# The first tile's key matmuls moved ahead of the second tile's transposes

## The chip, the cores and the metric

The kernel runs on one core of one Trainium2 chip. A core has five engines with instruction queues of their own: TensorE (matmuls, in the profile PE, with PEld for its weight loads), VectorE (DVE), ScalarE (ACT), GpSimd (POOL) and SyncE (SP, which here only issues transfers). Matmuls write to PSUM, which has 8 banks; VectorE and ScalarE carry results from there to SBUF. The metric is the device time of one execution in microseconds (us), as a median of several runs. The span of the profile is the time from the first to the last instruction, a little shorter.

## The reference, cut to what matters

The input `x` has 2048 rows (S) of 512 columns (D). The output is a gated sum of two branches of it:

```
q, k, v = x @ wqkv          # 32 heads of 16
phi(t)  = where(t > 0, t + 1, exp(t)) + 1e-6
kv      = phi(k)^T v        # per head, 16 x 16
z       = sum over rows of phi(k)
a       = (phi(q) kv) / (phi(q) . z + 1e-6) @ wo
h       = layernorm(x)
b       = (gelu(h^T @ w1 + b1) @ w2 + b2)^T      # mixes the rows
g       = sigmoid(sum(x * gate_w))
out     = g * a + (1 - g) * b
```

All inputs and the output are bf16. Of this, the change touches only how the first rows' keys `k = x @ wk` are started.

## The kernel before, in words

The rows are cut into 16 tiles of 128 (`NT`), the 512 columns into four chunks of 128 (`ND`). A matmul contracts over the partitions, so `k = x @ wk` needs x with its columns on the partitions: `xT`. For tiles 3 to 15 transposing DMAs (`load_xT`, L134) write `xT` directly. Those would come too late for the first three tiles (`HEADS = 3`), which TensorE transposes itself: `transpose_tile` (L202) multiplies each of the four 128x128 chunks of a tile with the identity, into one PSUM bank `pt`. VectorE then copies chunks 0 and 1 to `xT` (L209), and ScalarE chunks 2 and 3 (L210).

`k_part(t, ks)` (L224) runs the key matmuls of tile t for the chunks in `ks`; four of them, 128x128 by 128x512, add up to one bank `kacc`. `k_phi(t)` then calls `phi` (L212): an exp on ScalarE (L214), a min and an addition on VectorE (L215), and on VectorE again the sum with the positive part, which writes `pk` (L218). Next to these, `ln_step` takes the layer norm's statistics of a tile on VectorE (L238, L239).

The kernel is written under a manual schedule: each engine gets its instructions in the order of the calls in the program, and works them off in that order. An instruction waits for its inputs and for its output buffer, and whatever is behind it on the same engine waits with it. Tiles of PSUM come from one pool of 8 banks, in turn. The dependencies are kept per such tile; in the built program ScalarE's copy of `pt` waits for VectorE's copy of the same `pt`.

Loads: SyncE issues x's tiles 0, 1 and 2 one by one, then the transposing loads, the other tiles, and the weights; ScalarE issues the two halves of `wk` (chunks 0 and 1, chunks 2 and 3). Six matmuls on constants (`warm_up(6)`) keep TensorE at work until x's first tile is there.

The stretch around the change starts at L286: the transposes of tiles 0 and 1, the first two key matmuls of both, the transposes of tile 2, one `ln_step`, and then for tiles 0 to 2 the remaining key matmuls and the phi. After it comes the loop over tiles 3 to 15, in which the key matmuls of tile t alternate with `g_tile(t - 4)`, four matmuls of x against `pk` (`gacc`). Then follow the first products of the row mixing together with the queries (`uacc`, `qacc`), the rest of that product with the small attention matrices, and at last the output tiles (`aps`, `yps`).

Of the kernel before, what the change touches and what calls it, by code (L numbers as in the profile page):

```python
# [7 lines left out]
ACT = mybir.ActivationFunctionType  # L8
# [7 lines left out]
def kernel(  # L16
# [13 lines left out]
    nc = tc.nc  # L30
    P = nc.NUM_PARTITIONS
# [9 lines left out]
    ND = D // P  # L41
# [25 lines left out]
    def keep(shape, dtype, name):  # L67
        return persist.tile(shape, dtype, name=name, tag=name)

    def bank(name, dtype=FP32):  # L70
        return ps.tile([P, SC], dtype, name=name, tag="bank")

    xs = keep([P, NT, D], BF16, "xs")
    hs = keep([P, NT, D], BF16, "hs")
    xT = keep([P, ND, S], BF16, "xT")
# [17 lines left out]
    ident = keep([P, P], BF16, "ident")  # L93
# [18 lines left out]
    def mm(o, lhsT, rhs, start, stop, **kw):  # L112
        nc.tensor.matmul(o, lhsT=lhsT, rhs=rhs, start=start, stop=stop, **kw)  # L113
# [20 lines left out]
    def load_xT(t0, n):  # L134
# [14 lines left out]
        out=ident[:], in_=ident[:], compare_op=ALU.not_equal, fill=1.0, base=0,  # L149
# [5 lines left out]
        out=maskQ[:], in_=maskH[:].rearrange("p (a m) -> p m a", m=2), op=ALU.max, axis=AX.X  # L155
# [4 lines left out]
        out=xT[:, :, 3 * P : 3 * P + 2],  # L160
        in_=xs[:, 0, 0 : 2 * ND].rearrange("p (k c) -> p k c", k=ND),
# [10 lines left out]
    for c, (j0, nb) in enumerate(w1_chunks):  # L172
        w = wpool.tile([P, NT, FB * P], BF16, name="w1c", tag="wc")
        w1c.append(w)
        for t0 in range(0, NT, 8) if c < 3 else (0,):
            t1 = t0 + 8 if c < 3 else NT
            nc.sync.dma_start(
                out=w[:, t0:t1, : nb * P], in_=w1_view[:, t0:t1, j0 * P : (j0 + nb) * P]
# [15 lines left out]
    def warm_up(n, cols=SC):  # L194
        for _ in range(n):
            mm(wps[:, :cols], warm[:, 0:P], warm[:, :cols], True, True)
# [2 lines left out]
    nc.scalar.activation(out=act_warm[:], in_=ones_f[:], func=ACT.Exp)  # L199
    warm_up(6)  # L200

    def transpose_tile(t):  # L202
        pt = bank("pt")
        for k in range(ND):
            mm(pt[:, k * P : (k + 1) * P], xs[:, t, k * P : (k + 1) * P], ident[:], True, True)
        H = ND // 2
        src = pt[:].rearrange("p (k s) -> p k s", k=ND)
        dst = xT[:, :, t * P : (t + 1) * P]
        nc.vector.tensor_copy(out=dst[:, 0:H], in_=src[:, 0:H])  # L209
        nc.scalar.activation(out=dst[:, H:], in_=src[:, H:], func=ACT.Copy)  # L210

    def phi(dst, acc):  # L212
        e = work.tile([P, SC], BF16, name="e", tag="e", bufs=6)
        nc.scalar.activation(out=e[:], in_=acc[:], func=ACT.Exp)  # L214
        nc.vector.tensor_scalar(  # L215
            out=e[:], in0=e[:], scalar1=1.0, scalar2=PHI_EPS, op0=ALU.min, op1=ALU.add
        )
        nc.vector.scalar_tensor_tensor(  # L218
            out=dst, in0=acc[:], scalar=0.0, in1=e[:], op0=ALU.max, op1=ALU.add
        )  # L220
# [3 lines left out]
    def k_part(t, ks):  # L224
        if t not in kaccs:
            kaccs[t] = bank("kacc")
        for k in ks:
            mm(
                kaccs[t][:], xT[:, k, t * P : (t + 1) * P], wk_sb[:, k, :],
                k == 0, k == ND - 1,  # L230
            )

    def k_phi(t):
        phi(pk[:, t, :], kaccs.pop(t))
# [46 lines left out]
    def ln_step(u):  # L281
        ln_stats(u)
        if u % TPC == TPC - 1:
            ln_rstd(u // TPC)

    HEADS = 3  # L286
    transpose_tile(0)
    transpose_tile(1)
    for t in range(2):
        k_part(t, range(2))  # L290
    transpose_tile(2)
    ln_step(0)
    for t in range(HEADS):
        k_part(t, range(2 if t < 2 else 0, ND))
        k_phi(t)
    ln_step(1)
# [159 lines left out]
    for j in range(NB0, NF):  # L456
# [19 lines left out]
        out=gg[:], in0=gth[:], scalar1=0.5, scalar2=0.5, op0=ALU.mult, op1=ALU.add  # L476
    )
    nc.vector.tensor_scalar(
        out=c1[:], in0=gth[:], scalar1=-0.5, scalar2=0.5, op0=ALU.mult, op1=ALU.add
# [3 lines left out]
    for t in range(NT):  # L483
        c, tl = divmod(t, TPC)
        aps = bank("aps")
        for j in range(ND):
# [3 lines left out]
            out=a_sc[:], in_=aps[:], func=ACT.Identity,  # L490
            scale=gg[:, t : t + 1], bias=c2[:, t : t + 1],
        )
        for c0, W in ((0, D - P), (D - P, P)) if t == NT - 1 else ((0, D),):
            cs = slice(c0, c0 + W)
            yps = bank("yps")
            for f in range(NF):
# [6 lines left out]
                out=ot[:, :W], in0=yps[:, :W], scalar=c1[:, t : t + 1], in1=a_sc[:, cs],  # L503
# [35 lines left out]
```

## Time and profile before

| | |
|---|---|
| time, median of 3 runs | 164.42 us (164.37 to 164.69) |
| span of the profiled execution | 162.3 us |
| TensorE busy | 157.4 us, 97% |
| VectorE busy | 89.8 us, 55% |
| ScalarE busy | 63.1 us, 39% |
| landing of x's tiles 0, 1, 2 after their issue | 2.4, 3.1, 4.0 us |
| landing of the two halves of wk after their issue | 3.2, 3.8 us |
| granted TensorE clock | 1.0 |

How to read it: busy is the time in which an engine has at least one instruction under way. Matmuls are pipelined, so a row of them that starts every 0.216 us shows 0.38 us for each; the distance of the starts is what each costs in a dense row. The chain that ended last is followed back from the last instruction, at each step to what released it; its time stretches are the ones that set the end. In a timeline the brackets at the end of a line give the idle time of the engine ahead of it, and what ended it.

### The profile page before, as it was taken

To read this page: it belongs to the slowest core of one execution; us is meant where nothing else is said; L and a number is where in the kernel's file an instruction comes from. 1 tells how busy PE (TensorE), PEld (TensorE's weight loads), DVE (VectorE), ACT (ScalarE), POOL (GpSimd) and SP (SyncE) were. 2 spreads that over 40 slices of the span, in tenths; PEclk is the share of its full clock that TensorE was granted. 3 is DMA by queue.
4 is the path that set the end of the run, shared out by engine and by line. 5 is a ranking of instruction groups with operands and counts; after the bars stand their busy time and mean duration, and the time that the engine had idled before them with its cause. 6 is when DMAs were issued, how large, how long until landed. Compare 5 with 4: busy or idle time off the path is not lost.

```text
span 162.3 us, 2177 instructions
## 1 busy us (share of the span) xinstructions
PE 157.4 (97%) x819; PEld 72.2 (44%) x833; DVE 89.8 (55%) x212; ACT 63.1 (39%) x98; POOL 17.5 (11%) x34
## 2 busy tenths in 40 slices
PE   7899999999999999999999999999999999999993
PEld 2444444444444444444444444444444444444452
DVE  1699999967999999519995301256211111111112
ACT  3552294748677483112865113111122222111110
POOL 3000701200110000001415500050000000000000
DMA  5999999999910007600992699732000001110001
GB/s 156 239 220 231 277 321 325 379 385 386 358 30 0 0 0 233 219 4 0 284 325 88 201 326 313 278 128 71 32 32 32 32 32 42 48 43 33 32 32 32
DMA packets 30569, 25.18 MB, mean 155 GB/s; under 512 B 8480, under 2 KB 29984, under 8 KB 30560
## 3 DMA queue, kind: packets, MB, share of 16 engines
q1 hardware_dynamic: 28288, 21.89, 43.4%
q0 software_dynamic: 1440, 2.38, 5.4%
q10 hardware_dynamic: 832, 0.79, 1.5%
q8 instruction: 6, 0.10, 0.3%
q14 instruction: 3, 0.02, 0.0%
HBM read 21.11 MB, written 2.23 MB: 144 GB/s over the span
## 4 chain that ended last, share of the span: by engine, by line
PE 95%; DMA 2%; issue 1%; DVE 0%; SPq 0%
PE uacc L113 30%; PE yps L113 30%; PE gacc L113 8%; PE aps L113 8%; PE kacc L113 8%; PE qacc L113 8%; DMA xs<-in_A_x_dram 2%; PE denps L113 1%; PE pt L113 0%; PE kvps L113 0%; DVE xT L209 0%; SPq L129 0%; PE w2ps L113 0%; DVE ot L502 0%; PE pt L332 0%
## 5 line engine op out<-in xcount | busy, mean ns | idle before, releaser
L113 PE MATMUL uacc<-hs,w1c 128*128 128x512 bf16 x220 | 51.1, 379 | 0.2
L113 PE MATMUL yps<-uT,w2c 128*128 128x512 bf16 (+2 forms) x234 | 50.6, 366 | 0.2
L502 DVE SCALAR_TENSOR_TENSOR ot<-yps,c,a_sc 128x512 bf16<-128x512 f32 (+2 forms) x17 | 12.2, 719 | 44.7 <-PE yps L113 41.5
L113 PEld LDWEIGHTS <-w2c 128*128 128x128 bf16 x238 | 22.8, 98 | 25.9
L113 PEld LDWEIGHTS <-w1c 128*128 128x128 bf16 x224 | 21.8, 98 | 26.3 <-issue 0.2
L489 ACT ACTIVATE a_sc<-aps,c,gg 128x512 f32<-128x512 f32 x16 | 12.4, 777 | 46.7 <-PE aps L113 39.9
L326 ACT ACTIVATE uT<-uacc,bcol 128x512 bf16<-128x512 f32 x14 | 9.3, 688 | 21.7 <-PE uacc L113 21.7
L113 PE MATMUL qacc<-xT,wq_sb 128*128 128x512 bf16 x61 | 16.1, 379 | 0.2
L113 PE MATMUL aps<-W2sb,pqT 128*128 128x512 bf16 x63 | 16.2, 379 | 0.1
L113 PE MATMUL kacc<-wk_sb,xT 128*128 128x512 bf16 x63 | 16.1, 379 | 0.2
L113 PE MATMUL gacc<-pk,xs 128*128 128x512 bf16 x63 | 15.7, 379 | 0.0
L254 ACT ACTIVATE hs<-xs,nmr,rstd 128x512 bf16<-128x512 bf16 x16 | 12.8, 806 | 3.1 <-DVE nmr L248 3.1
L214 ACT ACTIVATE e<-qacc 128x512 bf16<-128x512 f32 x16 | 9.6, 597 | 9.2 <-PE qacc L113 9.2
L441 POOL DMA_DIRECT2D rex<-rd_dram x16 | 9.4, 601 | 22.5 <-DVE pqT L443 20.0
L214 ACT ACTIVATE e<-kacc 128x512 bf16<-128x512 f32 x16 | 9.3, 593 | 6.6 <-DVE mv L239 2.3
L218 DVE SCALAR_TENSOR_TENSOR pqT<-qacc,e 128x512 bf16<-128x512 f32 x16 | 11.1, 692 | 0.6
L218 DVE SCALAR_TENSOR_TENSOR pk<-kacc,e 128x512 bf16<-128x512 f32 x16 | 11.1, 692 | 0.6
L113 PEld LDWEIGHTS <-xs 128*128 128x128 bf16 x76 | 7.2, 100 | 9.4 <-DMA xs<-in_A_x_dram 1.6
L238 DVE BATCH_NORM_STATS2 stats<-xs 128x6 f32<-128x512 bf16 x16 | 10.9, 684 | 0.0
L215 DVE TENSOR_SCALAR e<-e 128x512 bf16<-128x512 bf16 x32 | 9.0, 281 | 2.3 <-ACT e L214 2.1
L428 DVE CUSTOM_DVE_ANT_0 junk<-xs,gw_b 128x512 bf16<-128x512 bf16 x16 | 9.8, 681 | 0.0
L279 DVE TENSOR_TENSOR zacc<-zacc,pk 128x512 f32<-128x512 f32 x14 | 9.6, 685 | 0.2
(61 smaller groups left out, 70.1 us busy)
## 6 DMA issues: line engine op xcount, KB each, us to landing
w1c<-in_B_w_dram SPq DMA_DIRECT2D x7, 1024.0 KB, 10.7
w2c<-in_B_w_dram SPq DMA_DIRECT2D x8, 896.0 KB, 5.9
rex<-rd_dram POOLq DMA_DIRECT2D x16, 128.0 KB, 4.0
out_dram<-ot SPq DMA_DIRECT2D x13, 128.0 KB, 1.7
xs<-in_A_x_dram SPq DMA_DIRECT2D x3, 512.0 KB, 4.6
wk_sb<-in_A_wqkv_dram ACTq DMA_DIRECT2D x2, 256.0 KB, 3.5
xs<-in_A_x_dram SPq DMA_DIRECT2D x4, 128.0 KB, 3.4
wq_sb<-in_A_wqkv_dram SPq DMA_DIRECT2D x1, 512.0 KB, 6.8
```

The costliest lines, as they stand in the source:

```text
L113: nc.tensor.matmul(o, lhsT=lhsT, rhs=rhs, start=start, stop=stop, **kw)
L214: nc.scalar.activation(out=e[:], in_=acc[:], func=ACT.Exp)
L215: nc.vector.tensor_scalar(out=e[:], in0=e[:], scalar1=1.0, scalar2=PHI_EPS, op0=ALU.min, op1=ALU.add)
L218: nc.vector.scalar_tensor_tensor(out=dst, in0=acc[:], scalar=0.0, in1=e[:], op0=ALU.max, op1=ALU.add)
L238: nc.vector.bn_stats(out=stats[:], in_=xs[:, t, :])
L254: nc.scalar.activation(out=hs[:, t, :], in_=xs[:, t, :], func=ACT.Identity, scale=rstd[:, t : t + 1], bias=nmr[:, t : t + 1],)
L279: nc.vector.tensor_tensor(out=zacc[:], in0=first, in1=pk[:, t, :], op=ALU.add)
L326: nc.scalar.activation(out=uT[:, j, :], in_=acc[:], func=ACT.Gelu_apprx_tanh, bias=bcol[:, j : j + 1])
L428: nc.vector.tensor_tensor_reduce(out=junk[:], in0=xs[:, t, :], in1=gw_b[:], scale=1.0, scalar=0.0, op0=ALU.mult, op1=ALU.add, accum_out=gp ...
L441: nc.gpsimd.dma_start(out=rex[:], in_=src.unsqueeze(1).to_broadcast([8, HEAD, SC]))
L489: nc.scalar.activation(out=a_sc[:], in_=aps[:], func=ACT.Identity, scale=gg[:, t : t + 1], bias=c2[:, t : t + 1],)
L502: nc.vector.scalar_tensor_tensor(out=ot[:, :W], in0=yps[:, :W], scalar=c1[:, t : t + 1], in1=a_sc[:, cs], op0=ALU.mult, op1=ALU.add,)
```

## The change

The change has three parts.

- `transpose_tile` is cut into `transpose_part`, which transposes a range of chunks into a bank of its own and copies it with one engine. A tile takes two banks where it took one, the first tile three.
- The first tile's chunks 0 and 1 are copied one by one by VectorE, so that the key matmul of chunk 0 need not wait for chunk 1.
- The order is another: the first two key matmuls of tile 0 come between the transposes of tiles 0 and 1; the other two, with the tile's phi, come ahead of the transposes of tile 2.

It is meant to give TensorE work while the second tile's rows are still under way, and to have the first phi early.

```diff
+    def transpose_part(t, k0, k1, on_act):
+        pt = bank("pt")
+        for k in range(k0, k1):
+            mm(pt[:, k * P : (k + 1) * P], xs[:, t, k * P : (k + 1) * P], ident[:], True, True)
+        src = pt[:, k0 * P : k1 * P].rearrange("p (k s) -> p k s", k=k1 - k0)
+        dst = xT[:, k0:k1, t * P : (t + 1) * P]
+        if on_act:
+            nc.scalar.activation(out=dst, in_=src, func=ACT.Copy)
+        else:
+            nc.vector.tensor_copy(out=dst, in_=src)
+
     def transpose_tile(t):
-        pt = bank("pt")
-        for k in range(ND):
-            mm(pt[:, k * P : (k + 1) * P], xs[:, t, k * P : (k + 1) * P], ident[:], True, True)
-        H = ND // 2
-        src = pt[:].rearrange("p (k s) -> p k s", k=ND)
-        dst = xT[:, :, t * P : (t + 1) * P]
-        nc.vector.tensor_copy(out=dst[:, 0:H], in_=src[:, 0:H])
-        nc.scalar.activation(out=dst[:, H:], in_=src[:, H:], func=ACT.Copy)
+        transpose_part(t, 0, ND // 2, False)
+        transpose_part(t, ND // 2, ND, True)
...
     HEADS = 3
-    transpose_tile(0)
+    transpose_part(0, 0, 1, False)
+    transpose_part(0, 1, 2, False)
+    transpose_part(0, 2, ND, True)
+    k_part(0, range(2))
     transpose_tile(1)
-    for t in range(2):
-        k_part(t, range(2))
+    k_part(1, range(2))
+    k_part(0, range(2, ND))
+    k_phi(0)
     transpose_tile(2)
     ln_step(0)
-    for t in range(HEADS):
+    for t in range(1, HEADS):
         k_part(t, range(2 if t < 2 else 0, ND))
         k_phi(t)
     ln_step(1)
```

## The prediction

> **What bounds the kernel now.** I read the page's busy shares first, then the chain that ended last in order of time, then the waits of TensorE's weight loads (each matmul's first half, so a stalled matmul shows there), and last the timeline of the first 10 us. The page:
>
> ```profile
> PE 157.4 (97%) x819; PEld 72.2 (44%) x833; DVE 89.8 (55%) x212; ACT 63.1 (39%) x98; POOL 17.5 (11%) x34
> ```
>
> TensorE is busy for 97% of the span, so little is to be had outside it, and any hole torn into it is paid in full. Where are its holes? The start of the chain (start us, length us, what):
>
> ```profile
> 1.27 3.08 DMA xs<-in_A_x_dram
> 4.35 0.05 issue
> 4.40 0.41 PE pt L113 x4
> 4.81 0.02 issue
> 4.83 0.44 DVE xT L209
> 5.27 0.05 issue
> 5.31 0.60 PE kacc L113 x2
> 5.92 0.28 PE pt L113 x4
> 6.20 3.45 PE kacc L113 x16
> ```
>
> It goes through the landing of x's second row tile (4.35), that tile's transposes, VectorE's copy of their first half to SBUF, and that tile's first two key matmuls at 5.31. From there on it names TensorE alone. The weight loads' waits over the whole run (total us, times, longest us):
>
> ```profile
> PEld L113 <- DMA xs<-in_A_x_dram: 1.6, 3, 0.7
> PEld L113 <- DVE xT L209: 0.6, 1, 0.6
> PEld L113 <- DVE kvT L345: 0.4, 1, 0.4
> ```
>
> The first two rows lie before 6 us; the third is a wait for the engine itself, in the middle of the kernel. So after 5.31 us nothing waits for a load or for VectorE long enough to swallow a delay. The timeline (start us, length us, engine, line, what):
>
> ```profile
> 4.03 0.43 DVE L209 CAST xT<-pt 128x256 bf16<-128x256 f32 x1 [0.66 <-PE pt L113]
> 4.49 0.38 ACT L210 ACTIVATE xT<-pt 128x256 bf16<-128x256 f32 x1 [1.17 <-DVE xT L209]
> 6.04 3.62 PE L113 MATMUL kacc<-wk_sb,xT 128*128 128x512 bf16 x16
> 6.24 0.42 DVE L209 CAST xT<-pt 128x256 bf16<-128x256 f32 x1 [0.98 <-PE pt L113]
> 6.58 0.68 DVE L238 BATCH_NORM_STATS2 stats<-xs 128x6 f32<-128x512 bf16 x1
> 6.98 1.58 ACT L214 ACTIVATE e<-kacc 128x512 bf16<-128x512 f32 x3
> 7.60 0.29 DVE L215 TENSOR_SCALAR e<-e 128x512 bf16<-128x512 bf16 x1
> 7.93 0.69 DVE L218 SCALAR_TENSOR_TENSOR pk<-kacc,e 128x512 bf16<-128x512 f32 x1
> 8.54 0.28 DVE L215 TENSOR_SCALAR e<-e 128x512 bf16<-128x512 bf16 x1
> ```
>
> Two things are to be seen. The third tile's copy on VectorE (6.24) stands ahead of the first phi (7.60 and 7.93). And 16 key matmuls run from 6.04 without a break: one starts every (3.62 - 0.38) / 15 = 0.216 us, so the third tile's first, the fifth of the row, starts at 6.04 + 4 x 0.216 = 6.90. That is the moment to compare with.
>
> **What the Trainium skill says.** "TensorE: Matmul & The Clock Gate", section "Architectural detail: the array is 16× 32×32, not 1× 128×128", has VectorE and ScalarE as strict FIFOs; the trace agrees, since every row of theirs stands in the order of the calls. The same page, "What's actually happening", says that TensorE runs at half rate until it has been busy for a window of about 3.4 us, and falls back after one idle window. The trace shows the first part: the first tile's transposes start 0.107 us apart from 3.36 on, the second's, from 4.40, about 0.06 apart. "VectorE: DVE Perf Modes", section "The TRN2 errata — SBUF-src ops pay a fixed extra latency per instruction", prices a copy out of PSUM at 120 cycles plus one per element at 0.96 GHz: 0.39 us for 256 elements, where the trace has 0.425.
>
> **The change, part by part.** Short names: T0, T1, T2 are the transposes of tiles 0 to 2, and Ki(0,1) the first two key matmuls of tile i. In the two built programs TensorE's order goes from T0, T1, K0(0,1), K1(0,1), T2, K0(2,3), K1(2,3), K2 to T0, K0(0,1), T1, K1(0,1), K0(2,3), T2, K1(2,3), K2. VectorE's goes from copy T0, copy T1, copy T2, stats, phi(0) to two copies of T0, copy T1, phi(0), copy T2, stats.
>
> *Banks.* Each part of a tile now has a PSUM bank of its own. ScalarE's copy then waits for TensorE and no longer for VectorE (4.49 becomes about 4.03), and VectorE's waits for two transposes rather than four: some 0.11 us earlier in T1.
>
> *First chunks.* A 128x128 copy is not in the trace. From above, the 0.425 us of 256 elements less 128 / 0.96 GHz = 0.133 gives 0.29; from below, the skill's price gives an estimate of (120 + 128) / 0.96 = 0.26. I take 0.29, as the page's price is short for 256 too. T0's transposes are untouched; the first ends at 3.67 (start 3.36, length 0.31). First copy 3.70 to 3.99, the second 3.91 to 4.20, as neighbours on VectorE overlap by 0.08 (7.93 + 0.69 = 8.62 against 8.54). The first half of wk, issued at 0.80, landed 3.2 us later, at 4.0. So K0(0) starts near 4.06, a copy's end to matmul costing 0.06 (5.25 to 5.31), and two matmuls of 0.216 let T1 begin at 4.50. The clock may still be at half rate: it rose somewhere between 3.68 and 4.40, so the loss is between nothing and (4.40 - 4.06) / 2 = 0.17. I take 0.08: T1 at 4.58, against 4.40 before.
>
> *Was that wait worth anything?* K1(0,1) must follow T1's copy: 4.58, the second transpose 0.06 later and 0.22 long, 0.03 to the copy, 0.425 for it, 0.06 on: 5.375, against 5.31. The hole before T1 is filled, but by work that used to fill the hole behind T1, and T1 now starts later. So this half yields nothing, and costs 0.07.
>
> *The new wait.* K1(0,1) and K0(2,3) take 4 x 0.216 = 0.86, to 6.24; their inputs are there (second half of wk at 1.3 + 3.8 = 5.1, ScalarE's copy of T0 long before). T2 takes 0.24 (5.80 to 6.04 before), to 6.48; its rows landed at 1.7 + 4.0 = 5.7. K1(2,3) takes 0.43, to 6.91. Next is K2(0,1), which waits for VectorE's copy of T2. In VectorE's queue that copy is now behind phi(0), and phi(0) needs K0's sum, through ScalarE's exp. K0's last matmul starts at 6.24 - 0.216 = 6.02 and ends at 6.40. Then: 0.04 to the exp (before, the fourth tile's last key matmul ended at 6.04 + 11 x 0.216 + 0.38 = 8.80, its exp began at 8.83), the exp 0.60, to 7.04; 0.03 and the min at 7.07; the next instruction 0.33 after it (7.60 to 7.93), 0.69 long, 7.40 to 8.09; the copy 0.08 before that end, at 8.01, 0.425 long, to 8.435; 0.06 to K2(0) at 8.50. TensorE stands from 6.91 to 8.50, with all its later work queued behind K2(0).
>
> *The sum.* K2(0) moves from 6.90 to 8.50: +1.60 us. Everything behind it is the same list of matmuls at the same pace. phi(1) and phi(2), pushed back by the copy and the stats, come about 0.7 later than before, TensorE 1.6 later, so no new wait is to be expected from VectorE; its extra work is 2 x 0.29 - 0.425 = 0.16 us, in time in which it waits anyway. The weights' loads come no later than before, so they are hidden better. 164.42 + 1.60 = 166.0.
>
> **The rivals.**
> *A slower start* (chance 0.10): K0(0) waits longer for wk or the clock. K0(0,1) stands ahead of T1, so every 0.1 us goes straight through. For it: the latest that wk can have come in the trace of before is 4.63, where K0(0) ran. From there T1 would be at 5.07 and all moves by 0.5 more: 166.5. Against: the landing in the trace is 4.0.
> *The clock falls back* (0.06): 1.6 us of idling could bring half rate; one window of 3.4 us at half rate costs an estimated 1.7 more (from the skill's window): 167.7. Against: the hole is under half a window, and the holes of 0.4 to 0.6 us before left no slow matmuls.
> *The delay is absorbed, or the early key matmuls pay* (0.06, the other side): if T1 still started at 4.40 and the copy of T2 were not in the way, K1(0,1) would gain the 0.11 us of the bank split: 164.3. For it: the chain of before begins with just these waits. Against: the order of VectorE's queue is fixed, and after 5.31 the chain holds no wait that could give 1.6 us back.
>
> **How the numbers follow.** The forecast itself has 0.78. Its own bounds: T1 not delayed at all gives 1.42, the half-rate clock at its worst and a little late wk give 1.8, and the times of before spread by 0.3. 165.5 to 166.6 holds that, takes in the slower start, and leaves out the clock's fall and the other side. Faster 0.03 and same 0.03 come from the last rival, slower 0.94 from all else.
>
> **What would show it.** Right: in the changed kernel the weight loads wait about 1.6 us in one piece for VectorE's copy of xT, ending near 8.5; the min of phi(0) starts near 7.1 and that copy near 8.0; K0(0) starts near 4.06 and K1(0) near 5.4; from 8.5 on TensorE is as dense as before. Wrong: the copy of T2 ahead of phi(0) on VectorE, no wait over 0.5 us after 6 us, a wait of some 0.5 us for wk ahead of 4.6, or key matmuls at 0.43 us apart after 8.5.

## The result, and the profile after

The changed kernel takes 165.70 us (median of 6, 165.34 to 165.97) against 164.39 (median of 6, 164.21 to 164.69): a ratio of 1.0075, with a 95% interval of 1.0056 to 1.0093. It is slower by 1.3 us; 1.6 was forecast. The profiled executions are 163.8 against 162.3 long.

The page's busy shares of the changed kernel:

```profile
PE 157.5 (96%) x819; PEld 72.2 (44%) x833; DVE 90.0 (55%) x213; ACT 63.4 (39%) x98; POOL 17.5 (11%) x34
```

TensorE works as long as before (157.5 against 157.4 us), in a longer span: the work is the same, a hole was added. The weight loads' waits over the whole run of the changed kernel (total us, times, longest us) say for whom:

```profile
PEld L113 <- DVE xT L211: 2.8, 3, 1.9
PEld L113 <- DMA xs<-in_A_x_dram: 0.6, 2, 0.3
```

Before, these rows held 0.6 and 1.6. The waits for x's rows shrank by 1.0, as the change meant, and those for VectorE's copy grew by 2.2, with one of 1.9 in one piece. The start of the chain that ended last, in order of time (start us, length us, what):

```profile
4.06 0.61 PE kacc L113 x2
4.67 0.28 PE pt L113 x2
...
4.97 0.43 DVE xT L211
...
5.45 1.05 PE kacc L113 x4
...
6.53 0.61 ACT e L219
...
7.16 0.30 DVE e L220
...
7.48 0.69 DVE pk L223
8.17 0.34 DVE xT L211
...
8.56 2.76 PE kacc L113 x12
```

Between 6.53 and 8.56 the chain leaves TensorE: exp, min and sum of phi(0), and only then the copy of T2, for which the third tile's key matmuls wait. Before, the chain named TensorE alone from 5.31 on, and those matmuls started at 6.90.

### The profile page after: what moved, and what is told of

Read it like the earlier page. It is cut to its first block, busy times and chain, and to the rows that moved or that the text cites. A ratio compares the mean times of both kernels' runs of the same rounds, so it can differ in the third digit from the quotient of the medians.

```text
span 163.8 us, 2178 instructions
## 1 busy us (share of the span) xinstructions
PE 157.5 (96%) x819; PEld 72.2 (44%) x833; DVE 90.0 (55%) x213; ACT 63.4 (39%) x98; POOL 17.5 (11%) x34
## 4 chain that ended last, share of the span: by engine, by line
PE 96%; DVE 1%; issue 1%; ACT 0%
PE uacc L113 29%; PE yps L113 29%; PE kacc L113 9%; PE aps L113 8%; PE qacc L113 8%; PE gacc L113 8%; PE wps L113 2%; DVE xT L211 1%; PE denps L113 1%; DVE pk L223 0%; ACT e L219 0%; PE kvps L113 0%; PE pt L113 0%; PE w2ps L113 0%; DVE ot L511 0%
## 5 line engine op out<-in xcount | busy, mean ns | idle before, releaser
L113 PEld LDWEIGHTS <-w2c 128*128 128x128 bf16 x238 | 22.8, 98 | 25.9
L113 PEld LDWEIGHTS <-xT 128*128 128x128 bf16 x64 | 6.1, 98 | 9.5 <-DVE xT L211 2.8
```

## Where 0.2 us came back

The third tile's key matmuls start 8.56 - 6.90 = 1.66 later, but the first matmul of the row mixing (`uacc`) only 34.47 - 33.00 = 1.47. The rest lies at the last `g_tile`. The timeline before (start us, length us, engine, line, what):

```profile
31.40 0.69 DVE L218 SCALAR_TENSOR_TENSOR pk<-kacc,e 128x512 bf16<-128x512 f32 x1
32.14 0.53 PEld L113 LDWEIGHTS <-xs 128*128 128x128 bf16 x3 [0.32 <-issue]
```

And after, the same place:

```profile
32.21 0.69 DVE L223 SCALAR_TENSOR_TENSOR pk<-kacc,e 128x512 bf16<-128x512 f32 x1
32.53 1.61 PEld L113 LDWEIGHTS <-xs 128*128 128x128 bf16 x8
```

Before, VectorE finished the last `pk` at 31.40 + 0.69 = 32.09, and TensorE's next weight load began at 32.14, after a gap that the profile puts down to "issue". TensorE could have been there at 31.94: its last matmul before began at 31.72, and one takes 0.216. So it waited 0.20 for VectorE, which had been at work since phi(0) with no gap over 0.04. After, the last `pk` is there at 32.21 + 0.69 = 32.90, and the four matmuls that need it are the last ahead of 34.47, so TensorE wants it only at 34.47 - 4 x 0.216 = 33.61: no gap. The forecast had held that no wait for VectorE was left that could give anything back.

The distance from the third tile's first key matmul to the first `uacc` matmul shows this wait in any of these kernels: 25.9 without it, 26.1 with it. The starts come from the timelines (in a merged row 0.216 apart), the times are medians, the ratio is to the kernel before as run beside it (164.24 to 164.39 us). The ratio weighs all executions, so a few long ones raise it above that of the medians:

| kernel | third tile's key matmuls | first uacc | distance | time us | ratio (95% interval) |
|---|---|---|---|---|---|
| before | 6.90 | 33.00 | 26.10 | 164.39 | |
| changed | 8.56 | 34.47 | 25.91 | 165.70 | 1.0075 (1.0056 to 1.0093) |
| 1: changed, phi(0) behind T2 | 6.98 | 33.03 | 26.05 | 164.57 | 1.0010 (0.9999 to 1.0020) |
| 2: before, phi(0) ahead of T2 | 8.62 | 34.53 | 25.91 | 165.60 | 1.0088 (1.0060 to 1.0116) |
| 3: before, K0(0,1) ahead of T1 | 7.43 | 33.52 | 26.09 | 164.80 | 1.0055 (1.0028 to 1.0082) |
| 4: before, cut transposes | 7.10 | 33.00 | 25.90 | 164.04 | 0.9981 (0.9969 to 0.9994) |
| 5: before, early statistics | 7.29 | 33.19 | 25.90 | 164.00 | 0.9985 (0.9974 to 0.9995) |
| 6: changed, early statistics | 9.03 | 34.94 | 25.91 | 165.48 | 1.0081 (1.0062 to 1.0100) |
| 7: combined | 7.63 | 33.53 | 25.90 | 164.19 | 0.9991 (0.9976 to 1.0006) |
| 8: changed, T2 copied by ScalarE | 8.15 | 34.06 | 25.91 | 164.83 | 1.0035 (1.0022 to 1.0047) |
| 9: cut transposes and early statistics | 6.84 | 32.74 | 25.90 | 164.11 | 0.9990 (0.9976 to 1.0005) |
| 10: changed, again | 8.40 | 34.31 | 25.91 | 165.86 | 1.0085 (1.0068 to 1.0102) |
| 11: as 1, with early statistics | 6.98 | 32.87 | 25.89 | 164.24 | 0.9997 (0.9985 to 1.0010) |

The starts are those of one execution each, the times those of many; that one execution and the median differ by up to 0.5, for much of which experiment 10 has a reason. Three of the 14 executions of version 3 took 166.5 to 166.8 us, one of version 2 took 167.06 and one of version 9 166.08; none of these was traced, and their cause stays open.

## Experiment 1: phi(0) behind T2

```diff
     k_part(0, range(2, ND))
-    k_phi(0)
     transpose_tile(2)
     ln_step(0)
+    k_phi(0)
     for t in range(1, HEADS):
```

> The changed kernel with one call moved: the first tile's phi comes behind the third tile's transposes and the statistics of the first tile. TensorE's order is that of the changed kernel, only VectorE's and ScalarE's is altered. Theory (the copy of T2 stands behind phi(0) on VectorE): that copy starts at about 6.65, the third tile's key matmuls at about 7.1 instead of 8.56, and the time is 164.4 to 164.7. Rival (the cost is that T1 stands behind the first key matmuls, or the order on TensorE as such): the third tile's key matmuls stay near 8.5 and the time near 165.7.

TensorE's order is untouched. The timeline:

```profile
6.50 0.42 DVE L211 CAST xT<-pt 128x256 bf16<-128x256 f32 x1 [1.24 <-PE pt L113]
6.85 0.68 DVE L243 BATCH_NORM_STATS2 stats<-xs 128x6 f32<-128x512 bf16 x1
...
7.66 0.26 DVE L220 TENSOR_SCALAR e<-e 128x512 bf16<-128x512 bf16 x1
```

The copy of T2 runs at 6.50 and the third tile's key matmuls at 6.98; 164.57 us. Of the 1.3 us all but 0.24 is gone with one call moved, and the interval of what is left reaches to nothing. So the place of phi(0) in VectorE's and ScalarE's queues is the cause, and not the order on TensorE.

## Experiment 2: phi(0) ahead of T2, alone

```diff
     transpose_tile(1)
     for t in range(2):
         k_part(t, range(2))
+    k_part(0, range(2, ND))
+    k_phi(0)
     transpose_tile(2)
     ln_step(0)
-    for t in range(HEADS):
+    for t in range(1, HEADS):
```

> The kernel before with one part of the change alone: the last two key matmuls of the first tile and its phi come ahead of the third tile's transposes; transposes, banks and copies stay as they were. Theory: the third tile's key matmuls start near 8.4 (8.56 less the 0.14 by which the changed kernel starts its second tile's key matmuls later), one wait of TensorE of about 1.5, and a time of 165.6 to 165.9. Rival (the first half of the change costs the time): no wait of over 0.3 after 6 us, and a time of 164.3 to 164.5.

The same fault, brought into the kernel before. Its chain:

```profile
7.54 0.69 DVE pk L218
8.23 0.34 DVE xT L209
...
8.62 2.76 PE kacc L113 x12
```

165.60 us: this part alone costs what the whole change costs. Experiments 1 and 2 settle it from both sides.

## Experiments 3 and 4: the other two parts alone

```diff
# 3
     transpose_tile(0)
+    k_part(0, range(2))
     transpose_tile(1)
-    for t in range(2):
-        k_part(t, range(2))
+    k_part(1, range(2))
     transpose_tile(2)
# 4: transpose_part and the new transpose_tile, nothing else
```

> The kernel before with the first two key matmuls of the first tile ahead of the second tile's transposes, and nothing else; one bank and one copy of two chunks as before. Theory: the copy of T0 ends at 4.46, these matmuls run from 4.5 to 4.95, T1 moves from 4.40 to about 4.95, and the second tile's key matmuls from 5.31 to about 5.85: +0.5, of which the wait of 0.2 near 32 us may give some back, so 164.6 to 164.95. Rival (work put into the hole ahead of T1 is gained): the second tile's key matmuls at 5.3 or earlier, the time 164.0 to 164.4.

> The kernel before with the cut transposes alone: two banks for a tile, each copied by one engine; order and two-chunk copies as before. Theory: VectorE's copy of T1 waits for two transposes and not four and starts 0.11 earlier, so the second tile's key matmuls start near 5.2, and the third tile's transposes then wait for their rows until 5.7: about 0.1 less in all, 164.2 to 164.4. Rival (more banks in the pool make matmuls wait for banks): a wait of TensorE between 6 and 12 us, and a time above 164.6.

The third kernel's chain:

```profile
4.51 0.65 PE kacc L113 x2
5.16 0.24 PE pt L113 x4
...
5.90 0.60 PE kacc L113 x2
```

The early key matmuls waited for T0's copy, T1 waited for them, and the second tile's key matmuls moved from 5.31 to 5.90: 164.80 us, 0.5 slower than the 164.33 beside it. The hole before T1 was filled and opened again behind it, larger. In the change the single copies and their banks bring the early matmuls forward by 0.45 (4.06 against 4.51), so that only 0.14 of this is left there (5.45 against 5.31).

The fourth was faster, by 0.3 us (164.04). Its timeline has the copy of T1 at 4.89, before the last transpose is over at 5.07, as expected. But the second tile's key matmuls began at 5.58 and not near 5.2: in this execution T1's transposes took 0.61 where the kernel before has 0.40, and the first tile's key matmuls behind them stood 0.42 apart. So the trace doesn't show the expected gain of 0.1. What it shows is another: the distance in the table is 25.90, the 0.20 wait is gone. With a bank of its own, ScalarE's copy of T2 no longer waits for VectorE's, so the exp and VectorE's long row start earlier against TensorE (the min of phi(0) 0.40 after the third tile's first key matmul, before it was 0.70).

## Experiments 5 and 6: is the gap at 32 us a wait for VectorE?

```diff
# 5, on the kernel before; 6 is the same on the changed kernel
     transpose_tile(1)
+    ln_step(0)
...
     transpose_tile(2)
-    ln_step(0)
+    ln_step(1)
...
-    ln_step(1)
```

> The kernel before with the layer norm statistics of tiles 0 and 1 one step earlier: tile 0's right behind the copy of T1, tile 1's behind the copy of T2, both in time in which VectorE waits. Theory (in the kernel before, VectorE's unbroken row of work from phi(0) to phi(15) ends 0.2 later than TensorE wants the last pk, near 32.1): the row is shorter by one pair of statistics, 0.86, pk of tile 15 is there near 31.2, TensorE's wait near 32 is gone, the first uacc matmul starts near 32.8 instead of 33.0, and the time is 164.05 to 164.25. Rival (that gap is no wait for VectorE): the gap stays and the time is 164.3 to 164.5.

> The changed kernel with the same two statistics one step earlier. Theory: in the changed kernel TensorE comes so late that it does not wait for the last pk, so nothing is gained: third tile's key matmuls near 8.55, first uacc matmul near 34.5, time 165.4 to 165.9; the distance to the kernel with the same edit but without the change is the full 1.5 to 1.7, not 1.3. Rival: it gains 0.2 as well, 165.1 to 165.5.

Two layer norm statistics are moved into time in which VectorE waits anyway, which shortens its row up to the last `pk` by one pair. In 5 the gap is gone:

```profile
30.98 0.69 DVE L218 SCALAR_TENSOR_TENSOR pk<-kacc,e 128x512 bf16<-128x512 f32 x1
31.03 1.82 PEld L113 LDWEIGHTS <-xs 128*128 128x128 bf16 x9
```

The distance falls from 26.10 to 25.90 and the time by 0.24 (164.00 against 164.24 beside it). In 6 nothing changes in the distance, and its 165.48 lies within the spread of the changed kernel. With the same edit in both, the change costs 165.48 - 164.00 = 1.48 instead of 1.31; the intervals of these two ratios are 0.2% to 0.4% wide, so the times agree with the 0.2 but do not measure it; the traces do. The first `uacc` matmul of 5 came later than expected (33.19), since in that execution everything started later (7.29).

## Experiment 8: the copy of T2 behind the exp only

```diff
-    transpose_tile(2)
+    transpose_part(2, 0, ND // 2, True)
+    transpose_part(2, ND // 2, ND, True)
```

> The changed kernel with the first half of T2 copied by ScalarE too, so that its copy is behind the exp of phi(0) but not behind VectorE's two instructions. Theory (the wait is as long as what stands ahead of the copy in its engine's queue): exp to 7.13, copy from 7.02 to 7.4, third tile's key matmuls near 7.5, half way between 6.9 and 8.56; with the wait near 32 gone or smaller, 164.6 to 165.0. Rival (phi(0) ahead of T2 costs the same whoever copies): 8.5, and 165.5 or more.

```profile
8.14 0.11 PEld L113 LDWEIGHTS <-xT 128*128 128x128 bf16 x2 [0.80 <-ACT xT L209]
```

TensorE was ready at 7.25 + 2 x 0.216 = 7.68 (the second tile's last two key matmuls began at 7.25) and started at 8.15: a hole of 0.47 where VectorE's queue made one of 8.56 - (6.55 + 2 x 0.216) = 1.58. The time, 164.83, is where it was expected; the start, 8.15 instead of 7.5, is not, as this execution was late by then: these last two key matmuls began at 7.25, in the changed kernel at 6.55, and less these 0.70 it would be 7.45. Experiment 10 has the reason. The cost follows the work that stands ahead of the copy: exp, min and sum, or the exp alone.

## Experiment 10: why the times come in two groups

> The changed kernel once more, in the company of the others and with more executions. Theory (the key matmuls put ahead of T1 run at half or at full clock, as the clock rises at another moment in each execution, and what they take longer goes to the end): times in two groups near 165.4 and 165.9, and a profile in which the start of the third tile's key matmuls, 8.56 where the two first ones took 0.61, is later by as much as these two take longer. Rival (the spread comes from the loads late in the kernel): the same start of the third tile's key matmuls with another time.

The six times are 165.37, 165.47 and 165.82 to 165.92; the first six had the same two groups. This run's profiled execution (165.37) is of the faster group, so its chain is set beside that of experiment 6 (166.00), which has the same order on TensorE:

```profile
4.06 0.60 PE kacc L113 x2
...
8.40 2.76 PE kacc L113 x12
```

```profile
4.17 1.01 PE kacc L113 x2
...
9.03 2.76 PE kacc L113 x12
```

9.03 - 8.40 = 0.63, and 166.00 - 165.37 = 0.63. In experiment 6 the two early key matmuls ran at half clock (1.01 instead of 0.60), and T1 behind them too; the first half of wk held them up by 0.1 (4.17 instead of 4.06). What happens before T1 is thus paid in full at the end. The other traces with these two matmuls at this place fit: in experiments 1 and 11 they took 0.59 and 0.61, and these executions (164.09 and 163.93) are among the fastest of their kernels; in experiment 8 they took 1.02, and its 165.11 is among the slower ones. The executions without a trace can't be looked into, so for the groups as a whole this cause is likely and not shown. A late load makes a smaller step of the same kind: in the first profiled execution of the changed kernel (165.53) the two matmuls had full clock (0.61), but x's second tile landed 3.3 us after its issue instead of 3.1, and the third tile's key matmuls began at 8.56, 0.16 later than here, as its time is 0.16 longer. The Trainium skill ("TensorE: Matmul & The Clock Gate", section "What's actually happening") has the window that decides on the clock running freely, so that the moment differs. The traces agree that it differs: T1's transposes were at full clock from 4.40 in the kernel before (0.40 for four), at half clock still near 5 in experiments 5 and 6 (0.61 and 0.63). The page has it vary by 0.5 us either way; the moments traced here lie further apart (last section).

## Experiments 7, 9 and 11: can the parts be put to use?

```diff
# 9: experiment 4 and experiment 5 together
# 11: experiment 1 with the statistics of experiment 5
# 7: as 9, with this order
     transpose_tile(0)
-    transpose_tile(1)
+    transpose_part(1, 0, 1, False)
+    transpose_part(1, 1, 2, False)
+    transpose_part(1, 2, ND, True)
     ln_step(0)
     for t in range(2):
         k_part(t, range(2))
-    transpose_tile(2)
+    k_part(0, range(2, ND))
+    transpose_part(2, 0, 1, False)
+    transpose_part(2, 1, 2, False)
+    transpose_part(2, 2, ND, True)
     ln_step(1)
+    k_phi(0)
-    for t in range(HEADS):
+    for t in range(1, HEADS):
...
```

> A version made from the findings: cut transposes with banks of their own; chunks 0 and 1 of tiles 1 and 2 (not of tile 0) copied one by one; order T0, T1, the first two key matmuls of tiles 0 and 1, the last two of tile 0, T2, the last two of tile 1; phi(0) behind T2's copies; statistics one step earlier. Theory: the second tile's key matmuls start near 5.1, the third tile's near 6.6 to 6.75 without a wait over 0.15, no wait near 32: 0.3 + 0.2 less than before, 163.8 to 164.1. Rival (the landing of x's tiles sets the pace anyway, or small copies cost more than they give): 164.2 or more.

> The kernel before with the two parts that helped by themselves: cut transposes with banks of their own, and the statistics of tiles 0 and 1 one step earlier; the order of the matmuls is that of before. Theory: the two gains have different causes (a copy that starts 0.1 earlier, a wait near 32 that is gone) and add up to 0.4 to 0.5: 163.75 to 163.95. Rival (they free the same wait): 164.0 to 164.1, no better than each alone.

> The changed kernel with phi(0) behind T2's copies and the statistics one step earlier: the early key matmuls are kept, the two faults found are mended. Theory (key matmuls ahead of T1 only move the hole): third tile's key matmuls at 7.0 to 7.2 or later, 0.1 to 0.4 slower than the version with banks and early statistics alone: 164.0 to 164.35. Rival (they are worth something once nothing else is in the way): 163.8 or less.

None reached the sum of its parts. In 7 the second tile's key matmuls did start at 5.0, but the first tile's last two, now ahead of T2, met the second half of wk:

```profile
1.30 5.20 DMA wk_sb<-in_A_wqkv_dram
...
6.55 0.59 PE kacc L113 x2
```

It took 5.2 us to land, where the kernel before had 3.8 and needed it only at 6.04. The times run from 163.56 to 164.72 with a median of 164.19: the best executions are the fastest seen, but the order makes the kernel depend on one more load, and it is not shown to be faster than before.

In 9 the two gains did not add up: 164.11, no better than either alone, as the rival said. They share the 0.20 wait (25.90 in all three), and either alone does away with it. Its trace has the third tile's key matmuls at 6.84 and no wait at 32. Versions 4 and 5 by themselves are faster than before by 0.19% (0.06 to 0.31) and 0.15% (0.05 to 0.26); which of the three is best can't be told from these runs.

In 11 the early key matmuls are kept and both faults are mended. At 164.24 it is level with the kernel before, and not faster than 5 or 9: the early key matmuls were worth nothing that can be seen.

## Why the prediction was right, and where its sizes were off

- *The new wait.* Right in mechanism and nearly in size. Forecast: exp at 6.44, min 7.07, sum 7.40, copy 8.01, third tile's key matmuls 8.50. Measured: 6.53, 7.16, 7.48, 8.09, 8.56. Experiments 1, 2 and 8 show it to be the cause.
- *The first half.* Right that it yields nothing: the second tile's key matmuls came at 5.45, forecast 5.375, before 5.31. T1 started at 4.64 for 4.58, but here because its rows landed at 4.6; the two key matmuls ahead of it had full clock (0.61), so the 0.08 put down to the clock was not what happened, and the near fit of this start is luck.
- *First chunks.* A copy was put at 0.29; two of them took 0.49 with their overlap, the second 0.20 after the first.
- *No wait swallows a delay.* This step failed, by 0.20. It was argued from the chain and from the weight loads' named waits; in the chain the gap at 32 us is only 0.04 us of "issue", and in the weight loads' waits it has no name, but stands under "issue". Corrected, the sum is 8.56 - 6.90 - 0.20 = 1.46, and the two profiled executions lie 165.53 - 164.05 = 1.48 apart.
- *1.48 and 1.31.* The profiled execution before was 0.34 under its median, the changed one 0.17 under its own. The difference of 0.17 is the rest; it is the spread of executions, not a saving of the change.
- *The clock.* The loss from half clock was bounded by one trace's moment of rising (4.40) at 0.17. The executions of experiments 6 and 8 had it later, and lost some 0.4 in the two matmuls alone. The range covered that by its rival of a slower start, which so is not a rival but a part of the executions. That the slower group at 165.9 lies so near the forecast of 166.0 is in part luck: if the clock makes that group, it has some 0.4 of clock where 0.08 was put, and it lacks the 0.20 that came back.
- *The clock falls back.* It did not: after the hole, 12 key matmuls took 2.76, which is full rate ((2.76 - 0.38) / 11 = 0.216).

## What to carry to other kernels

A consumer's input copy should stand ahead of any longer chain in the queue of the engine that makes it. On an engine that works in order, one short instruction put behind a chain that itself waits for TensorE makes TensorE wait for whatever is left of that chain once it has no other work, here 1.58 us. Work pulled ahead of a critical step to fill a hole is only free if it is over before that step's input arrives, in every execution and not just in the traced one. And before saying that nothing absorbs a delay, compare when the last input is finished with when the engine is ready, also where the profile says "issue".

## What the runs showed of the hardware that was not expected

- The moment at which TensorE goes to full clock differs between executions by over 1.7 us, with the same order on TensorE: by 4.06 in the changed kernel (two key matmuls that start there took 0.61), after 5.82 in experiment 8 (two that start there took 0.93). In the changed kernel two groups of times 0.5 us apart go with it.
- A hole of 1.58 us in TensorE's work did not bring half clock back.
- The second half of wk, 256 KB with the same loads issued ahead of it, took 3.7 us to land in experiment 10, 3.8 in the kernel before, 4.6 in the first trace of the changed kernel and 5.2 in experiment 7.
